# Key sums on TensorE and denominators read from PSUM for the first eight head pairs, in a plan where VectorE and GpSimd exclude each other

## The chip, the core and the metric

The kernel runs on one core of one Trainium2 chip. The metric is the device time of one execution in microseconds (us). Below, PE is TensorE, DVE is VectorE, ACT is ScalarE, POOL is GpSimd and SP is the engine whose queue issues the loads. SBUF is the working memory, PSUM the eight banks into which PE writes. "Pair" means two attention heads handled together.

## The reference

Linear attention with random features, and behind it a two-layer MLP; the MLP's weights arrive as 64-bit floats.

```python
q, k, v: [8, 8, 576, 64]        # batch, heads, sequence, head_dim; omega: [128, 64]

def phi(x):
    proj = np.einsum('bhsd,md->bhsm', x, omega)
    sq = np.sum(x * x, axis=-1, keepdims=True) / 2.0
    h = proj - sq
    h = h - np.max(h, axis=-1, keepdims=True)
    return np.exp(h) / np.sqrt(m)
q_p, k_p = phi(q_s), phi(k_s)                   # q, k scaled by 64**-0.25
kv = np.einsum('bhsm,bhsd->bhmd', k_p, v)
z = np.sum(k_p, axis=2)                         # the key sums
num = np.einsum('bhsm,bhmd->bhsd', q_p, kv)
den = np.einsum('bhsm,bhm->bhs', q_p, z)[..., None] + 1e-06
attn = num / den
x = attn.transpose(0, 2, 1, 3).reshape(4608, 512)
h = x @ w_in                                    # w_in [512, 2048]
out = (h / (1 + np.exp(-h))) @ w_out            # w_out [2048, 512]
```

## The kernel before

**Attention, one pair at a time (32 pairs, numbered n; four make a batch).** A pair's 1152 rows lie as nine chunks of 128: four of the first head, a middle chunk with 64 rows of each, four of the second. For keys and for queries PE projects the chunks into PSUM (`project`, L262, and the middle chunk apart, `project_mid`, L269). ACT squares the natural-layout copy and DVE sums it (`square_sum`, L254). DVE takes row maxima (`top`, L278 for four chunks, L276 for the middle one) and makes the shift (`shift`, L282 and L283, tiles `nbk` and `nbq`). ACT takes the exponential (L298).

**Key sums and denominators.** Before the change POOL adds the chunks of the exponentiated keys `hk` (`sums`, L318, L320, two of L323), PE adds over partitions with one product by a matrix of ones (`zsum`, L327), and ACT copies the result into SBUF as `zb` (`zcopy`, four copies). DVE multiplies `zb` with the exponentiated queries `hq` (`products`, L362, three instructions), sums the products (L369) and takes the reciprocal (L370). POOL scales the queries by it (`normal`, L375, three instructions), PE turns them (L381) and forms the numerators with the key-value matrix (`kv`, L343; `numer`, L399). ACT and DVE split the result into a high part `xh` (L413) and a low part `xl` (`x_low`, L418, two instructions, of 512 and of 64 columns). The pairs n < 8 (`DIRECT`) take their exponentials straight from PSUM.

**MLP.** There are nine row blocks t of 512 rows: the first 512 rows of each of the eight batches, and the remaining 64 of each together. Each block takes 16 steps f. A step is 12 products `x` by `w_in` into one bank (`stage1`, L495), two ACT instructions (L500, L501), one DVE subtraction (`g_low`, L505), and 12 products into four accumulator banks (`stage2`, L513). All of `stage1` of block 0 needs `xh` and `xl` of the pairs 0 to 3.

**Weights.** 32 tiles of weights are made from the 64-bit words. ACT makes the exponent part, DVE three instructions (`word`, L456, L458, L462, tile `w`), POOL two (`weight_high`, L476, and `weight_low`, L480). The step f of block 0 needs its own two tiles, so these 32 tiles are spread over the first part of the program.

**Order.** Each engine runs its instructions in the order written. That order comes from a list scheduler, `Plan.run`: each unit (a few instructions of one engine) has a duration, a key (its due time), the units that it comes after, and ring buffers and PSUM banks that it takes and frees. The scheduler repeatedly takes the unit that can start first, within 0.25 us the one with the lowest key. The PSUM banks are four `acc`, two `h` and two `att`. Before the MLP starts attention may use all of them; later only the two `att`:

```python
def bank_pools(u):
    pools = ["att"]
    if u["key"] < clock(LAG) - 1:
        pools.append("acc")
    if u["key"] < START_MLP - 1:
        pools.append("h")
```

Of the kernel before, what the change touches and what calls it, by code (L numbers as in the profile page):

```python
# [8 lines left out]
F32 = mybir.dt.float32  # L9
# [47 lines left out]
CALM = 0.5  # L57


def clock(step):  # L60
    return START_MLP + SLOW * min(step, 16) + STEP * max(step - 16, 0)


class Plan:
# [6 lines left out]
    def add(self, name, eng, dur, key, fn, after=(), order=(), alloc=(), free=(), banks=0, table=None, lat=0.0):  # L71
        u = dict(
            name=name, eng=eng, dur=dur, key=key, fn=fn, after=list(after), order=list(order), alloc=list(alloc),
            banks=banks, table=table, lat=lat,
        )
# [5 lines left out]
    def run(self):  # L81
        end, first = {}, {}
        slots = {r: [] for r in RINGS}
# [47 lines left out]
        while any(ready.values()):  # L131
            best = None
            for e, us in ready.items():
                pick, least = None, None
                for u in us:
# [21 lines left out]
                    t = max(t, free_at[e])  # L157
# [30 lines left out]
            order.append(u)  # L188
            for c in children.get(n, ()):
# [8 lines left out]
def attention_mlp(ctx: ExitStack, tc: tile.TileContext, qT, kT, qn, kn, v, om_in, w_in, w_out, out):  # L198
# [19 lines left out]
    prod = const.tile([P, NC, M + 1], F32, tag="prod", name="prod")  # L218
    nc.gpsimd.memset(prod, GUARD)
# [109 lines left out]

    def zcopy(n):  # L330
# [217 lines left out]
    for n in range(NWIN):  # L548
        calm = n < LEAD
        for i, who in enumerate("kq"):  # L550
# [6 lines left out]
            add(("raw",) + w, "SP", 0.42, at(n, i - 14, 8 + 10 * i - 32), lambda n=n, who=who: load_raw(n, who),  # L557
                order=prev("raw"), alloc=[(f"raw{who}", ("raw",) + w)], lat=1.3)
            before = [("nat", n, "k")] if i else ([("nat", n - 1, "q")] if n else [])
            add(("nat",) + w, "SP", 0.42, at(n, i - 13.5, 8.1 + 10 * i - 32), lambda n=n, who=who: load_nat(n, who),  # L560
# [3 lines left out]
            add(("ssum",) + w, "DVE", 0.78, at(n, 2 * i - 3, 14 + 10 * i - 32), lambda n=n, who=who: square_sum(n, who),  # L564
# [3 lines left out]
            add(pj, "PE", 1.5, at(n, 3 * i, o), lambda a, b, n=n, who=who: project(n, who, a, b), banks=2,  # L568
# [7 lines left out]
            for j in range(3):  # L576
                add(("top", n, who, j), "DVE", 0.3 if j == 2 else 0.7,
                    at(n, 3 * i + 1 + 0.1 * j, o + 1.2 + (4.5 if j == 2 else 0.1 * j)),
                    lambda n=n, who=who, j=j: top(n, who, j), after=[md if j == 2 else pj])
            if calm:  # L580
                add(("nb", n, who, 0), "DVE", 0.45, at(n, 3 * i + 1.5, 0), lambda n=n, who=who: shift(n, who, every),
                    after=[("top", n, who, j) for j in range(3)] + [("ssum",) + w], free=[("ss",) + w])
            else:
                add(("nb", n, who, 0), "DVE", 0.5, at(n, 0, o + 1.4), lambda n=n, who=who: shift(n, who, sides),
                    after=[("top", n, who, j) for j in range(2)] + [("ssum",) + w])
                add(("nb", n, who, 2), "DVE", 0.4, at(n, 0, o + 5.8), lambda n=n, who=who: shift(n, who, middle),
                    after=[("top", n, who, 2), ("ssum",) + w], free=[("ss",) + w])
# [15 lines left out]
        add(("v", n), "SP", 0.42, at(n, -8, 26 - 32), lambda n=n: load_v(n), order=[("v", n - 1)] if n else [],  # L603
            alloc=[("v", ("v", n))], lat=1.2)
# [3 lines left out]
        add(("sums", n), "POOL", 3.2, at(n, 6, 25), lambda n=n: sums(n), after=e["k"], order=[("sums", n - 1)] if n else [],  # L608
            alloc=[("t", ("t", n)), ("es", ("es", n))], free=[("h", n, "k"), ("t", n)])
        zn = ("z", n)  # L610
        add(zn, "PE", 0.45, at(n, 7, 32), lambda ps, n=n: zsum(n, ps), after=[("sums", n)], banks=1, free=[("es", n)])
        add(("zc", n), "ACT", 1.1, at(n, 7.1, 33.2), lambda n=n: zcopy(n), after=[zn], order=[("zc", n - 1)] if n else [],
            alloc=[("zb", ("zb", n))], free=[bk(zn)])
        merged = n > LEAD
        kn_ = ("kvnum", n - 1) if merged else ("kv", n)
        if not merged:
            add(("kv", n), "PE", 1.5, at(n, 6.5, 28.5), lambda ps, n=n: kv(n, ps), after=e["k"] + [("v", n)], banks=1,
# [3 lines left out]
        add(("ktt", n), "PE", 0.12, at(n, 6.7, 36.5), lambda ps, n=n: kv_turn(n, ps), after=[("kt", n)], banks=1,  # L621
# [3 lines left out]
        add(("prod", n), "DVE", 1.7, at(n, 8, 34.2), lambda n=n: products(n),  # L625
            after=e["q"] + [("zc", n)], order=[("den", n - 1)] if n else [], free=[("zb", n)])
        add(("den", n), "DVE", 1.6, at(n, 8.1, 34.4), lambda n=n: denom(n), after=[("prod", n)],
            alloc=[("den", ("den", n)), ("rd", ("rd", n))])
# [14 lines left out]
        dur = 1.4  # L643
        if follow:
# [3 lines left out]
            dur = 2.6  # L648
# [7 lines left out]
        add(("rest", n), "SP", 0.8, at(n, 20, 64), lambda n=n: keep_rest(n), after=[("xl", n, 0), ("xl", n, 1)], lat=0.2,  # L656
# [118 lines left out]
```

## Time and profile before

| | |
|---|---|
| device time, median of 3 runs | 1090.24 us (1089.62 to 1092.56) |
| profiled execution: its own time, its span | 1089.61 us, 1087.5 us |
| PE busy | 1040.2 us, 96% of the span |
| DVE, ACT, POOL busy | 572.1, 574.3, 254.6 us |
| the chain that ended last, by engine | PE 80%, DVE 9%, ACT 6%, DMA 2%, issue 2% |

The span runs from the first to the last instruction; 2.1 us of the execution's own time lie outside it. Busy time is an average over stages with different limits, so the stretches of the span are to be read one by one. Rows of the timeline give a start and a duration. Neighbouring rows of an engine overlap by some hundredths of a microsecond, so a cost in a row of instructions is best read from start to start.

### The profile page before, as it was taken

How to read it: one execution, taken by the hardware profiler on the slowest of the kernel's cores; microseconds unless marked ns; L12 is line 12 of the kernel's file. 1: busy time of each engine (PE TensorE's matmuls, PEld its weight loads, DVE VectorE, ACT ScalarE, POOL GpSimd, SP SyncE). 2: the span in 40 equal slices, each digit the busy share in tenths (PEclk: the TensorE clock that was granted, in tenths of full speed). 3: DMA queues.
4: the chain of work that ended last, by engine and by line, in shares of the span. 5: the costliest groups of instructions: out<-in, count | busy, mean ns of one | idle time of the engine just before them, and what ended most of it. 6: DMA issues, size and time to landing. Idle time of an engine off the chain costs nothing.

```text
span 1087.5 us, 16156 instructions
## 1 busy us (share of the span) xinstructions
PE 1040.2 (96%) x5900; PEld 825.2 (76%) x5900; DVE 572.1 (53%) x1109; ACT 574.3 (53%) x1077; POOL 254.6 (23%) x327
## 2 busy tenths in 40 slices
PE   5678998999999999999999999999999999999997
PEld 4456776677877778777877777777788778888886
DVE  6999988745555555545555555555555421111111
ACT  5677776565556555655556555655554543112111
POOL 3766655411222222121122211222222200000000
PEclk7868999999999999999999999999999999999999
DMA  7766777754435443544345444534442226333323
GB/s 274 248 220 228 271 249 243 238 176 141 141 123 176 128 126 118 175 141 130 123 133 172 126 136 141 180 122 137 130 157 89 65 83 213 97 97 126 107 97 97
DMA packets 66526, 167.84 MB, mean 154 GB/s; under 512 B 15632, under 2 KB 15760, under 8 KB 66448
## 3 DMA queue, kind: packets, MB, share of 16 engines
q1 hardware_dynamic: 65984, 166.23, 47.6%
q8 instruction: 47, 0.77, 0.3%
q10 hardware_dynamic: 464, 0.59, 0.2%
q14 instruction: 31, 0.25, 0.1%
HBM read 146.87 MB, written 19.92 MB: 153 GB/s over the span
## 4 chain that ended last, share of the span: by engine, by line
PE 80%; DVE 9%; ACT 6%; DMA 2%; issue 2%; POOL 0%; ACTq 0%; SPq 0%; DVEq 0%; POOLq 0%
PE ps_h L495 33%; PE ps_acc L513 32%; PE ps_att L262 5%; PE ps_att L343 3%; PE ps_att L381 2%; PE ps_att L399 2%; DVE w L458 1%; PE ps_att L327 1%; ACT L500 1%; DVE w L462 1%; PE ps_att L269 1%; DVE w L456 1%; DMA out<-ot 1%; DVE prod L362 1%; DMA wo_d<-wp 1%
## 5 line engine op out<-in xcount | busy, mean ns | idle before, releaser
L513 PE MATMUL ps_acc<-wo,gh 128*128 128x512 f32 x1152 | 369.0, 401 | 0.0
L500 ACT ACTIVATE gh<-ps_h 128x512 fp32r<-128x512 f32 x144 | 86.2, 599 | 308.4 <-PE ps_h L495 307.8
L505 DVE TENSOR_TENSOR gl<-ps_h,gh 128x512 fp32r<-128x512 f32 x144 | 97.9, 680 | 283.7 <-ACT ps_h L501 283.6
L513 PEld LDWEIGHTS ps_acc<-wo,gh 128*128 128x128 f32 x1152 | 206.2, 188 | 43.3
L495 PE MATMUL ps_h<-xh,wh 128*128 128x512 f32 x576 | 237.7, 413 | 0.3 <-ACT xh L413 0.3
L495 PE MATMUL ps_h<-xl,wh 128*128 128x512 f32 x576 | 225.5, 392 | 2.9 <-DVE xl L418 2.9
L495 PE MATMUL ps_h<-xh,wl 128*128 128x512 f32 x576 | 226.1, 393 | 0.0
L513 PE MATMUL ps_acc<-wo,gl 128*128 128x512 f32 x576 | 225.6, 392 | 0.0
L375 POOL TENSOR_TENSOR hq<-hq,rd 128x384 f32<-128x384 f32 x96 | 78.5, 846 | 380.0 <-DVE rd L370 375.3
L495 PEld LDWEIGHTS ps_h<-xh,wh 128*128 128x128 f32 x576 | 108.6, 189 | 24.8 <-ACT xh L413 0.5
L495 PEld LDWEIGHTS ps_h<-xl,wh 128*128 128x128 f32 x576 | 108.9, 189 | 24.1 <-DVE xl L418 3.3
L495 PEld LDWEIGHTS ps_h<-xh,wl 128*128 128x128 f32 x576 | 108.6, 188 | 24.5
L513 PEld LDWEIGHTS ps_acc<-wo,gl 128*128 128x128 f32 x576 | 108.1, 188 | 23.4
L318 POOL TENSOR_TENSOR t<-hk 128x256 f32<-128x256 f32 x64 | 48.8, 781 | 202.7 <-ACT hk L312 190.5
L312 ACT ACT_TABLE_LOAD x48 | 61.6, 1283 | 55.7 <-DVE hq L303 49.6
L501 ACT ACTIVATE ps_h<-ps_h 128x512 f32<-128x512 f32 x144 | 85.4, 593 | 0.0
L500 ACT ACT_TABLE_LOAD x56 | 71.8, 1283 | 22.7 <-PE ps_h L495 22.0
L278 DVE TENSOR_REDUCE mxq<-ps_att 128x4 f32<-128x512 f32 x57 | 36.9, 685 | 85.4 <-PE ps_att L262 85.4
L362 DVE TENSOR_TENSOR prod<-hq,zb 128x512 f32<-128x512 f32 (+1 forms) x96 | 53.0, 607 | 41.1 <-ACT zb L336 40.8
L250 ACT ACTIVATE nat<-nat 128x576 f32<-128x576 f32 x64 | 44.3, 700 | 23.4 <-DMA nat<-kn 18.6
L381 PE MATMUL ps_att<-ident,hq 128*128 128x128 f32 x261 | 41.0, 284 | 6.0 <-DVE hk L306 1.6
L278 DVE TENSOR_REDUCE mxk<-ps_att 128x4 f32<-128x512 f32 x55 | 35.5, 686 | 16.8 <-PE ps_att L262 16.8
(120 smaller groups left out, 1199.1 us busy)
## 6 DMA issues: line engine op xcount, KB each, us to landing
wo<-wo_d SPq DMA_DIRECT2D x144, 512.0 KB, 3.4
rawk<-kT SPq DMA_DIRECT2D x32, 352.0 KB, 3.0
rawq<-qT SPq DMA_DIRECT2D x32, 352.0 KB, 4.0
v<-v SPq DMA_DIRECT2D x32, 320.0 KB, 3.0
nat<-kn SPq DMA_DIRECT2D x32, 288.0 KB, 3.1
nat<-qn SPq DMA_DIRECT2D x32, 288.0 KB, 3.3
wraw<-w_in SPq DMA_DIRECT2D x16, 512.0 KB, 4.1
wraw<-w_out SPq DMA_DIRECT2D x16, 512.0 KB, 4.8
```

The costliest lines, as they stand in the source:

```text
L262: nc.tensor.matmul(ps[:, i * M : (i + 1) * M], raw[r, o : o + P], oms[r], start=True, stop=True)
L278: nc.vector.tensor_reduce(m[:, 5 * j : 5 * j + 4], ps.rearrange("p (c m) -> p c m", m=M), AX.X, ALU.max)
L312: nc.scalar.activation(h, h, AF.Exp)
L318: nc.gpsimd.tensor_tensor(t[:, j], e[:, 5 * j : 5 * j + 2], e[:, 5 * j + 2 : 5 * j + 4], ALU.add)
L362: nc.vector.tensor_tensor(prod[:, c, :M], e[:, c], zb[:, j].unsqueeze(1).broadcast_to([P, hi - lo, M]), ALU.mult)
L375: nc.gpsimd.tensor_tensor(e[:, c], e[:, c], rd[:, c].unsqueeze(2).broadcast_to([P, 3, M]), ALU.mult)
L381: nc.tensor.transpose(ps[:, i * P : (i + 1) * P], T["h", n, "q"][:, 3 * g + i], ident)
L495: nc.tensor.matmul(ph, w[:, k, :], x, start=k == 0 and n == 0, stop=k == NK - 1 and n == 2)
L500: nc.scalar.activation(gh, ph, AF.Silu)
L501: nc.scalar.activation(ph, ph, AF.Silu)
L505: nc.vector.tensor_tensor(gl, T["ph", t, f], T["gh", t, f].bitcast(F32), ALU.subtract)
L513: nc.tensor.matmul(T["po", t][j], g[:, js], w, start=f == 0 and n == 0, stop=f == NF - 1 and n == 2)
```

## The change

Four things change.

1. For the pairs n < 8, `sums`, `zsum` and `zcopy` are gone. `zsum_direct` lets PE sum the keys itself: ten products of 128x128 with ones (for the middle chunk with `sides_of`, ones in one half of the partitions) accumulate in one bank.
2. For the same pairs `denom_direct` replaces `products` and `denom`: ten times a product and a sum in one DVE operation, one input from SBUF and one straight from that PSUM bank. Each is two instructions in the built program, the operation and a read of its accumulator. The bank is freed when the last of them is done. For n >= 8 `denom` does nine of these with both inputs in SBUF, in place of three products and one sum.
3. The scheduler knows a "port": POOL's units and the DVE units marked `port` (the shifts, the weight words, the denominators of n >= 8) do not overlap in the plan. It also charges PE more after a gap. Many durations in its table are new.
4. `shift_keys` moves the keys of some early units by fixed pseudo-random amounts.

```diff
+SHIFTS = (1000, 1001, 1004, 1005, 1007, 1011, 1020, 1026, 1056, 1068, 1094, 1152, 1161,)
+def shift_keys(units):
+    early = [u for u in units if u["key"] < 235]
+    for seed in SHIFTS:
+        r = random.Random(seed)
+        part, wide = ((0.02, 6.0), (0.06, 3.0), (0.2, 1.5))[seed % 3]
+        for u, d in [(u, r.gauss(0, wide)) for u in early if r.random() < part]:
+            u["key"] += d
...
-                    t = max(t, free_at[e])
+                    t = max(t, free_at[e], port if u["port"] else 0.0)
...
+            if e == "PE":
+                if t - free_at[e] > 2.5:
+                    warm = t + 4.0
+                if t < warm:
+                    dur *= 1.7
             free_at[e] = t + dur
+            if u["port"]:
+                port = t + dur
...
-    prod = const.tile([P, NC, M + 1], F32, tag="prod", name="prod")
-    nc.gpsimd.memset(prod, GUARD)
+    sides_of = const.tile([P, 2, P], F32, tag="sides", name="sides")
+    nc.gpsimd.memset(sides_of, 0.0)
+    for j in range(2):
+        nc.gpsimd.memset(sides_of[j * D : (j + 1) * D, j], 1.0)
+    prod = const.tile([P, NC, M], F32, tag="prod", name="prod")
...
+    def zsum_direct(n, ps):
+        e = T["h", n, "k"]
+        for j in range(2):
+            nc.tensor.matmul(ps[:, j * M : (j + 1) * M], sides_of[:, j], e[:, MID], start=True, stop=False)
+            for i in range(4):
+                nc.tensor.matmul(ps[:, j * M : (j + 1) * M], ones, e[:, 5 * j + i], start=False, stop=i == 3)
+        T["z", n] = ps
+
+    def denom_direct(n):
+        e, z = T["h", n, "q"], T.pop(("z", n))
+        den = new("den", [P, NC])
+        for c in range(NC):
+            for j in range(2) if c == MID else [int(c > MID)]:
+                r = slice(j * D, (j + 1) * D) if c == MID else slice(0, P)
+                nc.vector.tensor_tensor_reduce(
+                    out=prod[r, c], in0=e[r, c], in1=z[r, j * M : (j + 1) * M], scale=1.0, scalar=GUARD, op0=ALU.mult,
+                    op1=ALU.add, accum_out=den[r, c : c + 1],
+                )
+        T["rd", n] = rd = new("rd", [P, NC])
+        nc.vector.reciprocal(rd, den)
...
-    def products(n):
+    def denom(n):
         e, zb = T["h", n, "q"], T.pop(("zb", n))
-        for j, (lo, hi) in enumerate(((0, 4), (4, 5), (5, 9))):
-            c = slice(lo, hi)
-            nc.vector.tensor_tensor(
-                prod[:, c, :M], e[:, c], zb[:, j].unsqueeze(1).broadcast_to([P, hi - lo, M]), ALU.mult
+        den = new("den", [P, NC])
+        for c in range(NC):
+            j = (c >= MID) + (c > MID)
+            nc.vector.tensor_tensor_reduce(
+                out=prod[:, c], in0=e[:, c], in1=zb[:, j], scale=1.0, scalar=GUARD, op0=ALU.mult, op1=ALU.add,
+                accum_out=den[:, c : c + 1],
             )
-
-    def denom(n):
-        den = new("den", [P, NC])
         T["rd", n] = rd = new("rd", [P, NC])
-        nc.vector.tensor_reduce(den, prod, AX.X, ALU.add)
         nc.vector.reciprocal(rd, den)
...
-            add(("ssum",) + w, "DVE", 0.78, at(n, 2 * i - 3, 14 + 10 * i - 32), lambda n=n, who=who: square_sum(n, who),
+            add(("ssum",) + w, "DVE", 0.76, at(n, 2 * i - 3, 14 + 10 * i - 32), lambda n=n, who=who: square_sum(n, who),
...
+        if n < DIRECT:
+            add(zn, "PE", 2.3, at(n, 6.2, 31), lambda ps, n=n: zsum_direct(n, ps), after=e["k"], order=[("mid", n, "q")],
+                banks=1, free=[("h", n, "k")])
...
+        if n < DIRECT:
+            add(("den", n), "DVE", 2.8, at(n, 8, 34.2), lambda n=n: denom_direct(n), after=e["q"] + [zn],
+                order=[("den", n - 1)] if n else [], alloc=[("den", ("den", n)), ("rd", ("rd", n))], free=[bk(zn)])
...
+    shift_keys(plan.units.values())
```

On POOL this is the program's start before, from the first key sums (`t`, `es`) on; `hq<-hq,rd` is the scaling of the queries, `wh`, `wl` and `wp` are the weight tiles.

```order
L318 TENSOR_TENSOR t<-hk 128x256 x2
L320 TENSOR_TENSOR es<-t 128x256
L323 TENSOR_TENSOR es<-es,hk 64x128 x2
L375 TENSOR_TENSOR hq<-hq,rd 128x384 x3
L476 CAST wh_324<-w_233 128x512
L480 TENSOR_TENSOR wl_325<-w_233,wh_324 128x512
L318 TENSOR_TENSOR t<-hk 128x256 x2
L320 TENSOR_TENSOR es<-t 128x256
L323 TENSOR_TENSOR es<-es,hk 64x128 x2
L476 CAST wh_404<-w_322 128x512
```

On POOL the same place now:

```order
L419 TENSOR_TENSOR hq<-hq,rd 128x384 x3
L520 CAST wh_312<-w_230 128x512
L524 TENSOR_TENSOR wl_313<-w_230,wh_312 128x512
L520 CAST wh_357<-w_306 128x512
L524 TENSOR_TENSOR wl_358<-w_306,wh_357 128x512
L520 CAST wp<-w_303 128x512
```

The key sums of the pairs have left POOL; scaling and weights follow each other directly.

On DVE this is the first pair's denominator before (`prod`, `den`, `rd`) and what follows it.

```order
L458 SCALAR_TENSOR_TENSOR w_233<-wre,w_233 128x512
L362 TENSOR_TENSOR prod<-hq,zb 128x4x128
L362 TENSOR_TENSOR prod<-hq,zb 128x128
L362 TENSOR_TENSOR prod<-hq,zb 128x4x128
L369 TENSOR_REDUCE den<-prod 128x9
L370 RECIPROCAL rd<-den 128x9
L254 TENSOR_REDUCE sqk<-nat 128x9
L282 TENSOR_TENSOR nbk<-mxk,sqk 128x9
L283 SCALAR_TENSOR_TENSOR nbk<-nbk,sqk 128x9
L254 TENSOR_REDUCE sqq<-nat 128x9
```

On DVE the end of the first pair's denominator now, and what follows it (`ps_att` is the PSUM bank with the key sums).

```order
L369 ISA prod,den<-hq,ps_att 128x128
L369 ISA den 128x1
L374 RECIPROCAL rd<-den 128x9
L303 TENSOR_REDUCE mxq<-ps_acc 128x4
L303 TENSOR_REDUCE mxq<-ps_h 128x4
L502 SCALAR_TENSOR_TENSOR w_230<-wre,w_230 128x512
L506 SCALAR_TENSOR_TENSOR w_230<-wraw,w_230 128x512
L279 TENSOR_REDUCE sqk<-nat 128x9
L307 TENSOR_TENSOR nbk<-mxk,sqk 128x9
```

The second pair's query maxima now stand behind the first denominator, and the two halves of a denominator's work (operation and accumulator read) alternate.

On PE this is the row from the fourth step of block 0 on in which the key sums of pair 5 stand now (`ps_att` from `hk`), between two quarters of a `stage2`.

```order
L557 MATMUL ps_acc<-wo,gl 128x512
L294 MATMUL ps_att<-oms,rawq 128x128
L358 MATMUL ps_att<-hk,sides 128x128
L360 MATMUL ps_att<-hk,ones 128x128 x4
L358 MATMUL ps_att<-hk,sides 128x128
L360 MATMUL ps_att<-hk,ones 128x128 x4
L557 MATMUL ps_acc<-wo,gh 128x512 x2
```

Five such groups of ten (pairs 0 to 4) stand ahead of the long run of `stage1` products that opens block 0, three (pairs 5 to 7) behind it.

## Rows read from the trace of the kernel before

**Rows 1.** Windows: stretch, busy us of each engine, PE clock, DMA share, GB/s.

```profile
0.00:90.00 90.00, 57.34 (x406) 41.03 (x407) 80.08 (x136) 59.42 (x178) 51.85 (x64) 0.75 0.74 250
90.00:210.00 120.00, 111.65 (x638) 85.65 (x639) 110.52 (x177) 85.42 (x170) 75.20 (x78) 0.99 0.74 248
210.00:1000.00 790.00, 789.28 (x4499) 630.99 (x4498) 370.16 (x780) 411.52 (x695) 127.52 (x187) 1.00 0.43 134
```

**Rows 2.** Timeline of DVE, first and last rows ahead of the long run.

```profile
5.66 0.75 DVE L254 TENSOR_REDUCE sqk<-nat 128x9 f32<-128x576 f32 x1 [4.66 <-ACT nat L250]
...
16.30 1.29 DVE L278 TENSOR_REDUCE mxq<-ps_acc 128x4 f32<-128x512 f32 x2 [2.01 <-PE ps_acc L262]
...
86.51 0.68 DVE L418 TENSOR_TENSOR xl<-ps_acc,xh 128x512 fp32r<-128x512 f32 x1
```

**Rows 3.** Timeline of POOL, one key sum and one weight.

```profile
10.86 0.72 POOL L318 TENSOR_TENSOR t<-hk 128x256 f32<-128x256 f32 x1 [8.59 <-ACT hk L298]
...
13.49 1.11 POOL L323 TENSOR_TENSOR es<-es,hk 64x128 f32<-64x128 f32 x2
...
26.02 1.59 POOL L480 TENSOR_TENSOR wl<-w,wh 128x512 fp32r<-128x512 f32 x1
```

**Rows 4.** Timeline of DVE beside those two.

```profile
10.96 0.65 DVE L282 TENSOR_TENSOR nbq<-mxq,sqq 128x9 f32<-128x9 f32 x1
...
26.52 1.64 DVE L462 SCALAR_TENSOR_TENSOR w<-wraw,w 128x512 uint32<-128x512 uint32 x1
```

**Rows 5.** Timeline of DVE, undisturbed: maxima and a shift.

```profile
8.85 0.28 DVE L276 TENSOR_REDUCE mxk<-ps_acc 128x1 f32<-128x128 f32 x1
9.16 0.17 DVE L282 TENSOR_TENSOR nbk<-mxk,sqk 128x9 f32<-128x9 f32 x1
...
9.45 1.28 DVE L278 TENSOR_REDUCE mxq<-ps_acc 128x4 f32<-128x512 f32 x2
10.65 0.28 DVE L276 TENSOR_REDUCE mxq<-ps_h 128x1 f32<-128x128 f32 x1
```

**Rows 6.** Timeline of DVE, undisturbed: one denominator.

```profile
18.52 1.50 DVE L362 TENSOR_TENSOR prod<-hq,zb 128x512 f32<-128x512 f32 x3
...
21.44 0.22 DVE L370 RECIPROCAL rd<-den 128x9 f32<-128x9 f32 x1
21.58 0.70 DVE L254 TENSOR_REDUCE sqk<-nat 128x9 f32<-128x576 f32 x1
```

**Rows 7.** Timeline of DVE, undisturbed: a low part and a sum of squares.

```profile
31.23 0.68 DVE L418 TENSOR_TENSOR xl<-ps_acc,xh 128x512 fp32r<-128x512 f32 x1
...
31.96 0.74 DVE L254 TENSOR_REDUCE sqk<-nat 128x9 f32<-128x576 f32 x1
32.62 0.67 DVE L278 TENSOR_REDUCE mxk<-ps_acc 128x4 f32<-128x512 f32 x1
```

**Rows 8.** Timeline of DVE, undisturbed: the three steps of a weight.

```profile
78.20 0.41 DVE L456 TENSOR_SCALAR w<-wraw 128x512 uint32<-128x512 uint32 x1
...
79.98 0.28 DVE L276 TENSOR_REDUCE mxq<-ps_att 128x1 f32<-128x128 f32 x1
```

**Rows 9.** Timeline of PE: products of 128x128, and the start of the long run.

```profile
11.86 2.40 PE L343 MATMUL ps_acc<-hk,v 128*64 128x128 f32 x20 [0.55 <-ACT hk L298]
...
34.12 0.49 PE L269 MATMUL ps_att<-oms,rawq 128*128 128x128 f32 x2
34.36 0.48 PE L495 MATMUL ps_h<-xh,wh 128*128 128x512 f32 x1
...
91.20 0.77 PE L495 MATMUL ps_h<-xh,wh 128*128 128x512 f32 x1
```

**Rows 10.** Timeline of PE: one key sum of before, and one `kv` later.

```profile
66.42 0.67 PE L327 MATMUL ps_att<-es,ones 128*128 128x256 f32 x2 [1.22 <-DVE xl L418]
66.93 0.39 PE L269 MATMUL ps_acc<-oms,rawk 128*128 128x128 f32 x2
...
144.44 1.31 PE L343 MATMUL ps_att<-hk,v 128*64 128x128 f32 x20
```

More of the change, by code (lines that the diff above doesn't have):

```diff
@@ L1 @@
+import random
 from contextlib import ExitStack
@@ L69, in __init__, with add @@
         self.freed_by = {}
-    def add(self, name, eng, dur, key, fn, after=(), order=(), alloc=(), free=(), banks=0, table=None, lat=0.0):
+    def add(self, name, eng, dur, key, fn, after=(), order=(), alloc=(), free=(), banks=0, table=None, lat=0.0, port=False):
         u = dict(
             name=name, eng=eng, dur=dur, key=key, fn=fn, after=list(after), order=list(order), alloc=list(alloc),
-            banks=banks, table=table, lat=lat,
+            banks=banks, table=table, lat=lat, port=port or eng == "POOL",
         )
@@ L79, in add, with run @@
             self.freed_by.setdefault(i, []).append(name)
-    def run(self):
+    def run(self, until=None):
         end, first = {}, {}
+        port, warm = 0.0, 0.0
         slots = {r: [] for r in RINGS}
@@ L188, in run @@
             order.append(u)
+            if n == until:
+                return t
             for c in children.get(n, ()):
@@ L580, in attention_mlp @@
             if calm:
-                add(("nb", n, who, 0), "DVE", 0.45, at(n, 3 * i + 1.5, 0), lambda n=n, who=who: shift(n, who, every),
-                    after=[("top", n, who, j) for j in range(3)] + [("ssum",) + w], free=[("ss",) + w])
-            else:
[L584 to L587, printed above, removed]
+                add(("nb", n, who, 0), "DVE", 0.36, at(n, 3 * i + 1.5, 0), lambda n=n, who=who: shift(n, who, every),
+                    after=[("top", n, who, j) for j in range(3)] + [("ssum",) + w], free=[("ss",) + w], port=True)
+            else:
+                add(("nb", n, who, 0), "DVE", 0.36, at(n, 0, o + 1.4), lambda n=n, who=who: shift(n, who, sides),
+                    after=[("top", n, who, j) for j in range(2)] + [("ssum",) + w], port=True)
+                add(("nb", n, who, 2), "DVE", 0.34, at(n, 0, o + 5.8), lambda n=n, who=who: shift(n, who, middle),
+                    after=[("top", n, who, 2), ("ssum",) + w], free=[("ss",) + w], port=True)
             for j in range(3):
@@ L655, in attention_mlp @@
                 lambda n=n, i=i: x_low(n, i), after=[("xh", n, i)], free=[bk(nm, i)])
-        add(("rest", n), "SP", 0.8, at(n, 20, 64), lambda n=n: keep_rest(n), after=[("xl", n, 0), ("xl", n, 1)], lat=0.2,
+        add(("rest", n), "SP", 0.75, at(n, 20, 64), lambda n=n: keep_rest(n), after=[("xl", n, 0), ("xl", n, 1)], lat=0.2,
             free=[("x", t, k)])
     def weight(i, key, src, last, more=()):
-        add(("wl",) + i, "SP", 0.42, key - 12, lambda: load_weight(src, i), order=[("wl",) + last] if last else [],
+        add(("wl",) + i, "SP", 0.36, key - 12, lambda: load_weight(src, i), order=[("wl",) + last] if last else [],
             alloc=[("wraw", ("wraw",) + i)], lat=2.1)
@@ L664, in weight @@
         for s in range(3):
-            add(("wd",) + i + (s,), "DVE", (0.5, 0.78, 0.75)[s], key - 2 + 0.1 * s, lambda s=s: word(i, s),
+            add(("wd",) + i + (s,), "DVE", (0.43, 0.7, 0.7)[s], key - 2 + 0.1 * s, lambda s=s: word(i, s),
                 after=([("wd",) + i + (s - 1,), ("re",) + i] if s else [("wl",) + i]),
@@ L680, in attention_mlp @@
         last = ("out", f)
-        add(("keep", f), "SP", 0.42, clock(f + LAG) + 4, lambda f=f: keep_weight(f), after=[("wlo", "out", f)], lat=2.1,
+        add(("keep", f), "SP", 0.36, clock(f + LAG) + 4, lambda f=f: keep_weight(f), after=[("wlo", "out", f)], lat=2.1,
             free=[("wp", f)])
```

48 lines of the change are left out of this document (24 added, 24 removed).

## Prediction

> **What bounds the kernel now.** I read the busy time by stretches first [rows 1]. From 210 us on PE is busy for 789.3 of 790 us: nothing that other engines do there can move the end. From 90 to 210 us it idles 8.35 us, and from 0 to 90 us 32.7 us, at a mean granted clock of 0.75. So only two things can change the time: the moment at which the long run of MLP products starts (91.20 us [rows 9]), and the work and gaps of PE behind it. Then I asked what holds that moment back. The run needs `xl` of pair 3, which DVE writes at 86.51 us [rows 2]; DVE is busy for 80.1 of the first 90 us [rows 1], and the longest wait in that stretch behind its first instruction is 2.0 us [rows 2]. The start is a queue of DVE instructions.
>
> That busy time isn't all work. The `shift` at 10.96 us takes 0.65 us and ends at 11.61, just behind POOL's addition that ends at 11.58; the same form takes 0.17 us when POOL rests [rows 3 to 5]. The weight word at 26.52 us takes 1.64 us; POOL's subtraction beside it runs until 27.61 [rows 3, 4], and what remains of the word behind that, 0.55 us, is less than the 0.6 or so that a quiet one takes. So some DVE operations stand still until POOL's current instruction is over, and this counts as busy. Reductions (0.60 us from start to start) and `xl` do not stretch.
>
> How much is it? By the written order, DVE does the following ahead of pair 3's `xl`, priced from start to start in quiet places [rows 5 to 8]: 13 sums of squares of 0.66, 22 maxima of 0.60, 10 middle maxima of 0.31, 13 shifts of 0.29, 9 weights of 1.78 and one first step more (0.45), 4 denominators of 3.06, one set of products (1.53), 3 low parts of 0.73: 61.1 us. It really takes 86.51 - 5.66 = 80.85 us, 2.0 of them idle. Some 17.7 us are collisions with POOL.
>
> **The change, part by part.**
>
> *DVE ahead of the long run.* The new order has ahead of pair 3's `xl`: 11 sums of squares, 20 maxima, 10 middle maxima, 11 shifts, 9 weights and 1.6 us of two begun ones, 3 low parts and a bit, 4 denominators. Without the denominators that is 7.3 + 12.0 + 3.1 + 3.2 + 17.6 + 2.3 = 45.5 us.
>
> A direct denominator is ten operations on 128 elements that read PSUM, ten accumulator reads and a reciprocal. No row shows the operation. Below stands the middle maximum, 128 elements from PSUM, started over 0.19 us if the next one needn't wait (0.31 less the wait), so 10 x 0.19 + 0.2 = 2.1 us. Above stands the same maximum at its full 0.28 us [rows 5] with 0.17 us for each read (the duration of an operation on nine elements [rows 5]) and a reciprocal: 10 x 0.45 + 0.2 = 4.7 us. I take 0.28 for each operation with its read hidden in the overlap, and 0.14 for the reciprocal (21.44 to 21.58 [rows 6]): 2.9 us, hardly less than the 3.06 of before. Four of them make 11.8 and the total 57.3 us. [...]
>
> *Collisions.* POOL's key sums go for pairs 0 to 4: one takes from 10.86 to 14.60 us [rows 3], five some 18.7 of POOL's 51.9 busy us [rows 1]. If collisions shrink with POOL's work, 17.7 becomes 11.3 us; if the new plan really keeps the two apart, 0. Nothing enforces the plan while it runs, so I take 6. The rows already show which operations are spared: the low part reads one input from PSUM and one from SBUF and keeps 0.68 us [rows 2, 7], the shift reads two from SBUF and stretches [rows 4]; the direct denominator is of the first kind. [...]
>
> *Waits.* With less of its own work DVE reaches operations whose input isn't ready. [...] I take 6 us for the idle of this stretch, between the 2 of now and 10.
>
> So `xl` of pair 3 starts at 5.66 + 57.3 + 6 + 6 = 75.0 instead of 86.5 us: 11.5 us earlier.
>
> *PE.* A product of 128x128 at the full clock takes 0.24 us from start to start (34.12 to 34.36 [rows 9]), ten 2.4 us; the key sum that goes took 0.51 (66.42 to 66.93 [rows 10]). Each pair costs PE 1.9 us more. Five of eight lie ahead of the long run, in the 32.7 idle us. Three lie behind it and count in full: 5.7 us. Six transposes also move behind the start, 0.8 us. Together 6.5 us later.
>
> *Gaps from 90 to 210 us.* The 8.35 us [rows 1] come from a DVE that is 92% busy there. Its 22 remaining weights and its shifts lose less to POOL, so gaps should shrink; against that, the bank with the key sums is now held until the denominator is done, and attention has two banks by then. Bounds: all 8.35 gone, or 6 us more (three pairs at 2). I take 4 us less.
>
> *What costs nothing.* ACT is spared four copies a pair and is 66% busy in the first 90 us. In the pairs n >= 8 DVE's denominators change, but DVE has 420 idle us of 790 there [rows 1]; cover gone, it would take some 17 us more per pair (420 over 24 pairs) before DVE were full. Loads: DMA works at a share of 0.74 for 90 us [rows 1]; the same bytes in 79 us ask 0.84, which leaves it the later bound. The three POOL fills of `sides_of` run in the first microseconds, where POOL rests until 10.86 [rows 3].
>
> **Sum.** Against the profiled execution: span 1087.5 - 11.5 + 6.5 - 4 = 1078.5 us, with the 2.1 us outside the span 1080.6. The median of the runs lies 0.6 us above that execution, so I forecast 1081 us, 0.8% faster. What this measurement can tell from no change is about 0.3%, 3.3 us: faster ends at 1087, slower begins at 1093.5.
>
> **The rivals.**
>
> *The collisions vanish* as planned and the gaps behind the start close: 6 + 4.35 us more, 1071 us. For it: each collision in the rows pairs a DVE operation with a POOL operation that the new order can set apart. Against it: order isn't time, and any late input shifts the two queues against each other.
>
> *The denominators are dear on DVE.* If each accumulator read costs its own start, four denominators take 7 us more: 1088 us. For it: five DVE instructions of a denominator become 21. Against it: small operations do overlap by some hundredths here.
>
> [...]
>
> **Chances and range.** 0.45 for my forecast (1075 to 1087), 0.17 for vanished collisions (1064 to 1075), 0.21 for dear denominators (1085 to 1092), 0.17 for a cold TensorE (1092 to 1100). Faster holds the first two and a quarter of the third, 0.67; same the rest of it and the edge of the last, 0.17; slower 0.16. The range from 1067 to 1095 leaves out about 0.05 below (all the low bounds at once) and 0.12 above.
>
> **What would show it.** Right: the long run starts at 77 to 82 us; shifts and weight words on DVE are near 0.17 and 0.42 to 0.69 us for the most part; the direct denominator takes some 2.9 us from its first operation to its reciprocal, whatever POOL does; PE's idle from the start to 210 us is near 4 us; the ten products take 2.4 us at the full clock. Wrong: DVE idle of over 10 us ahead of the start, with PE's key sums as what ended it (cold TensorE); denominators of over 4 us; weight words of over 0.9 us on average (the plan doesn't keep the engines apart); or idle on PE behind 210 us, where I assume none.

## The result and the profile after

The changed kernel takes 1076.95 us (median of 4 runs, 1074.47 to 1078.38). The kernel before takes 1090.94 us in the same comparison (1089.62 to 1092.56). The ratio is 0.9869, with a 95% interval from 0.9845 to 0.9893: 1.3% faster. The forecast was 1081 us, in a range from 1067 to 1095. The profiled execution after took 1076.36 us with a span of 1074.6 us; before, the span was 1087.5 us.

Over the whole span PE is busy for 6.5 us more than before (1046.7 instead of 1040.2 us) and idle for 19.4 us less (27.9 instead of 47.3 us). The windows of the kernel after answer to [rows 1]; the fourth line is the stretch from the new start of the long run to 210 us. Columns: stretch, its length, busy us of PE, PEld, DVE, ACT and POOL, each with its instructions, granted clock, DMA share, GB/s.

```profile
0.00:90.00 90.00, 71.24 (x562) 56.96 (x563) 79.78 (x234) 63.51 (x174) 38.96 (x48) 0.91 0.78 268
90.00:210.00 120.00, 116.25 (x695) 93.53 (x694) 91.73 (x234) 83.41 (x155) 55.64 (x57) 0.97 0.76 252
210.00:1000.00 790.00, 789.35 (x4484) 630.82 (x4483) 347.90 (x1090) 410.85 (x694) 125.83 (x184) 1.00 0.42 134
75.20:210.00 134.80, 129.01 (x763) 103.30 (x764) 106.16 (x269) 97.31 (x185) 64.86 (x66) 0.97 0.73 243
```

PE does 71.2 us of work in the first 90 us instead of 57.3, at a granted clock of 0.91 instead of 0.75. Behind 210 us nothing changed. DVE is as busy in the first 90 us as before, but gets much further in them, and POOL has 12.9 us less to do. The chain that ended last now lies on PE for 90%, by engine (before: PE 80%, DVE 9%, ACT 6%):

```profile
PE 90%; DVE 4%; ACT 2%; DMA 1%; issue 1%; POOL 0%; ACTq 0%; SPq 0%; DVEq 0%
```

The timeline of DVE after shows the first denominator (its first operation and the first read of its accumulator, then its reciprocal and the row behind), and the low part of pair 3.

```profile
14.15 0.29 DVE L369 CUSTOM_DVE_ANT_0 prod<-hq,ps_att 128x128 f32<-128x128 f32 x1 [0.88 <-ACT hq L323]
14.36 0.08 DVE L369 DVE_READ_ACCUMULATOR2_ANT den<- 128x1 f32 x1
...
16.57 0.22 DVE L374 RECIPROCAL rd<-den 128x9 f32<-128x9 f32 x1
16.70 0.63 DVE L303 TENSOR_REDUCE mxq<-ps_acc 128x4 f32<-128x512 f32 x1
...
72.63 0.68 DVE L462 TENSOR_TENSOR xl<-ps_att,xh 128x512 fp32r<-128x512 f32 x1
```

A denominator takes 16.70 - 14.15 = 2.55 us. Its operations start 0.21 us apart though each is shown with 0.28 us, and the reads of the accumulator lie inside that overlap. The low part starts at 72.63 instead of 86.51 us [rows 2].

The timeline of PE after has the key sums of the first pair, at a granted clock of 1.00, those of the second, and the start of the long run. Two groups of ten products are shown, each from its first row to the row behind it; the last row is the first product of the run.

```profile
11.52 0.46 PE L358 MATMUL ps_att<-hk,sides 128*128 128x128 f32 x2 [0.65 <-ACT hk L323]
...
13.92 0.33 PE L389 MATMUL ps_acc<-hk,v 128*64 128x128 f32 x2
...
26.10 0.63 PE L358 MATMUL ps_acc<-hk,sides 128*128 128x128 f32 x2
...
29.66 0.65 PE L443 MATMUL ps_att<-en,kw 128*64 128x512 f32 x2
...
75.20 0.48 PE L539 MATMUL ps_h<-xh,wh 128*128 128x512 f32 x1
```

Ten products took 2.40 us at 11.52, and 3.56 us at 26.10, where the stretch from 20 to 30 us has a granted clock of 0.57. Taken in stretches of 1 us, the clock shows two levels in this trace, 1.00 in 1045 and 0.50 in 21 of 1075, and something between in nine; from 20 to 28 us it is 0.50. The long run starts at 75.20 us, 16.0 us earlier [rows 9]. From there to the end it now takes 999.4 us, before 996.3. The windows from the start of the long run to the end, before and after:

```profile
91.20:1087.50 996.30, 981.68 (x5491) 783.27 (x5489) 490.86 (x973) 514.44 (x899) 201.52 (x263) 1.00 0.46 146
```

```profile
75.20:1074.60 999.40, 988.18 (x5552) 791.58 (x5552) 464.06 (x1375) 522.70 (x906) 190.69 (x250) 1.00 0.46 146
```

PE works 6.5 us longer there and idles 3.4 us less (11.2 instead of 14.6 us).

Does DVE still collide with POOL? Rows of POOL after, and below them rows of DVE beside them.

```profile
29.20 1.60 POOL L524 TENSOR_TENSOR wp<-w,wp 128x512 fp32r<-128x512 f32 x1
...
45.59 0.61 POOL L520 CAST wp<-w 128x512 fp32r<-128x512 f32 x1 [2.01 <-DVE w L506]
46.28 1.29 POOL L524 TENSOR_TENSOR wp<-w,wp 128x512 fp32r<-128x512 f32 x1
```

```profile
29.70 1.65 DVE L506 SCALAR_TENSOR_TENSOR w<-wraw,w 128x512 uint32<-128x512 uint32 x1
...
45.65 0.28 DVE L369 CUSTOM_DVE_ANT_0 prod<-hq,ps_acc 128x128 f32<-128x128 f32 x1
...
47.10 0.28 DVE L369 CUSTOM_DVE_ANT_0 prod<-hq,ps_acc 128x128 f32<-128x128 f32 x1
```

The weight word at 29.70 us waits out POOL's subtraction, 1.65 us instead of 0.69. The denominator from 45.44 us on runs through two POOL instructions, and each of its operations keeps 0.28 us.

I went through all rows of DVE up to 210 us in this way. A row counts as beside POOL if at least a tenth of it overlaps a row of POOL, and what it takes over its quiet duration (0.17 for a shift, 0.41, 0.69 and 0.69 for the words of a weight, 0.51 on average for a product of the old denominator) is its stretch. The sums are worked out from the two timelines:

| | rows that can stretch | of these beside POOL | stretch up to 210 us | ahead of pair 3's low part |
|---|---|---|---|---|
| before | 179 | 112 | 42.9 us | 17.7 us |
| after | 156 | 61 | 21.2 us | 9.1 us |

The first word of a weight has a single input in SBUF, and it stretches too: here (first DVE, then POOL) it takes 1.51 us instead of 0.41, beside a subtraction of POOL that ends at 127.26.

```profile
126.03 1.51 DVE L500 TENSOR_SCALAR w<-wraw 128x512 uint32<-128x512 uint32 x1
```

```profile
125.64 1.62 POOL L524 TENSOR_TENSOR wl<-w,wh 128x512 fp32r<-128x512 f32 x1
```

Of the 80 direct operations, 21 lie beside POOL. They take 0.282 us on average, and the 59 others take 0.283 us.

### The profile page after: what moved, and what is told of

It reads as the page before. It is cut to its first block, busy times and chain, and to the rows that moved or that the text cites. A ratio compares the mean times of both kernels' runs of the same rounds, so it can differ in the third digit from the quotient of the medians.

```text
span 1074.6 us, 16797 instructions
## 1 busy us (share of the span) xinstructions
PE 1046.7 (97%) x6044; PEld 838.8 (78%) x6044; DVE 529.4 (49%) x1573; ACT 572.3 (53%) x1049; POOL 220.4 (21%) x289
## 4 chain that ended last, share of the span: by engine, by line
PE 90%; DVE 4%; ACT 2%; DMA 1%; issue 1%; POOL 0%; ACTq 0%; SPq 0%; DVEq 0%
PE ps_acc L557 37%; PE ps_h L539 36%; PE ps_att L287 5%; PE ps_att L389 3%; PE ps_att L425 3%; PE ps_att L443 2%; PE ps_att L294 1%; DVE prod L369 1%; PE ps_att L352 1%; PE ps_att L360 1%; DVE w L502 1%; DMA wo<-wo_d 1%; DMA rawq<-qT 0%; ACT hk L323 0%; PE ps_acc L287 0%
## 5 line engine op out<-in xcount | busy, mean ns | idle before, releaser
L343 POOL TENSOR_TENSOR t<-hk 128x256 f32<-128x256 f32 x48 | 34.4, 738 | 199.1 <-ACT hk L337 199.1
L409 DVE CUSTOM_DVE_ANT_0 prod<-hq,zb 128x128 f32<-128x128 f32 x216 | 47.8, 288 | 38.9 <-ACT zb L382 38.9
L275 ACT ACTIVATE nat<-nat 128x576 f32<-128x576 f32 x64 | 44.4, 697 | 14.6 <-DMA nat<-kn 10.5
L429 ACT COPY en<-ps_att 128x384 f32<-128x384 f32 x89 | 40.5, 480 | 7.0 <-PE ps_att L425 5.4
```

The source lines that it names most:

```text
L275: nc.scalar.activation(nat, nat, AF.Square, scale=SCALE * 0.5**0.5)
L409: nc.vector.tensor_tensor_reduce(out=prod[:, c], in0=e[:, c], in1=zb[:, j], scale=1.0, scalar=GUARD, op0=ALU.mult, op1=ALU.add, accum_out= ...
L429: nc.scalar.copy(T["en", n][:, 3 * g * P : 3 * (g + 1) * P], T.pop(("t", n, g))[:, : 3 * P])
```

## The experiments

Each was run in five rounds against the kernel before, whose median was 1089.62, 1089.55 and 1088.70 us in the three groups of runs. So ratios are compared. "Start" is the start of pair 3's low part on DVE (before 86.51 us), "idle" that of PE from 90 to 210 us (before 8.35 us). The stretch is that of the rows named above; fused operations with both inputs in SBUF, which it leaves out, add 1.5 us in e3n and 2.3 us in e5n.

| | us | ratio to before | start | idle | stretch up to 210 us |
|---|---|---|---|---|---|
| the change | 1076.95 | 0.9869 (0.9845 to 0.9893) | 72.63 | 3.75 | 21.2 |
| e1 new operations, old plan | 1085.16 | 0.9956 (0.9939 to 0.9973) | 75.05 | 7.1 | 25.8 |
| e2 without shift_keys | 1083.76 | 0.9948 (0.9931 to 0.9965) | 73.87 | 6.5 | 21.8 |
| e9 without it and without port | 1080.98 | 0.9928 (0.9910 to 0.9945) | 80.6 | 6.3 | 24.4 |
| e3n without it, key sums on POOL | 1090.83 | 1.0016 (1.0006 to 1.0027) | 78.0 | 13.2 | 27.6 |
| e5n without it, direct for n < 5 | 1085.13 | 0.9964 (0.9951 to 0.9976) | 73.0 | 11.6 | 28.2 |
| e8n without it, sums copied to SBUF | 1079.37 | 0.9908 (0.9891 to 0.9925) | 80.6 | 3.7 | 22.8 |
| e4 before, shorter key sums | 1081.65 | 0.9924 (0.9906 to 0.9943) | 81.30 | 5.1 | 28.5 |
| e7 the change, idle work on POOL | 1080.22 | 0.9917 (0.9903 to 0.9930) | 75.38 | 5.5 | 27.7 |
| e10 before, idle work on PE | 1098.85 | 1.0090 (1.0076 to 1.0103) | 89.96 | 10.3 | 41.0 |

My theory was that POOL's key sums hold up DVE, and DVE the long run. Its rivals were that the plan, not the operations, brings the gain; that the shorter way to the denominator alone brings it; and that TensorE's clock does. The times of e2, e3, e4, e7, e8n and e10 fell into none of the ranges that I had written down for them.

**e1: the operations without the plan.** The new operations, with the scheduler, the durations and the keys of before. Two of the lines in which it differs from the changed kernel; the gap rule and the new durations are gone as well.

```diff
-                    t = max(t, free_at[e], port if u["port"] else 0.0)
+                    t = max(t, free_at[e])
...
-    shift_keys(plan.units.values())
```

> The new operations in the scheduler of before: key sums by TensorE and direct denominators for the first eight pairs, but no port rule, no gap rule, no shifted keys and the old durations for everything that is not new. If the gain comes from taking the key sums off GpSimd (five of 3.7 us ahead of the long run, so about a third fewer collisions and a shorter way to each denominator), the long run of MLP products starts at 80 to 86 us instead of 91.2 and the time is 1081 to 1087 us. If the gain comes from the new order alone, the start stays near 90 us and the three late key sums on TensorE make it 1094 to 1097 us.

The start came to 75.05 us, nearly where the whole change has it. But only a third of the gain in time came with it. PE idles 7.1 us from 90 to 210 us and 4.9 us from 210 to 1000 us (after: 3.75 and 0.65), in the later stretch for low parts of DVE alone (the time in total, the number of waits and the longest):

```profile
PE ps_att L330 <- DVE xl L440: 4.9, 5, 2.3
```

PE is also busy for 3.9 us longer than after (1050.6 us), although its mean clock is higher (0.992 instead of 0.988); why stays open.

**e2: the plan without the shifted keys.**

```diff
-    shift_keys(plan.units.values())
```

> The changed kernel without the shifted keys; port rule, gap rule and durations stay. If operations and port rule carry the gain, the start of the long run moves by at most 4 us from 75.2 and the time is 1075 to 1082 us. If the shifted keys carry it (an order tuned unit by unit), the start is at 84 us or later and the time 1086 us or more.

0.52% faster than before instead of 1.31%. So 0.8% hang on the shifted keys, more than half of the gain, although the start is only 1.2 us later. The windows of this run, the first from its start of the long run on:

```profile
75.95:210.00 134.05, 126.63 (x729) 99.06 (x727) 105.67 (x269) 91.92 (x172) 66.59 (x69) 0.96 0.73 244
...
210.00:1000.00 790.00, 788.33 (x4492) 629.97 (x4493) 350.41 (x1100) 411.06 (x693) 126.19 (x185) 1.00 0.42 135
```

Over its whole span of 1083.3 us PE idles 27.5 us, as after (27.9), but is busy for 9.1 us longer on the same 6044 instructions. Most of that goes with the clock: PE is busy for 31.4 us at the lower of the two levels, 0.50, after for 18.1 us. In the key sum at 26.10 us after, instructions start every 0.21 us at that level and every 0.11 us at 1.00, so 13.3 us more at the lower level cost some 6 us, as an estimate. In the stretches around its waits (PE busy for 7.98 of 10 us from 140 on and 7.18 from 160 on) and just behind them the granted clock is 0.80 to 0.86 in three of four slices. The remaining 3 us I can't place. Nor is the clock all of it: of the six executions of e2 the one with the highest mean clock (0.991) takes 1081.54 us, and the slowest of the change, at 0.987, takes 1078.38 us.

shift_keys draws its numbers in the order of the early units. Where a variant adds or takes away units, the same seeds move other keys. Three kernels (e3, e5 and e8) were first run with shift_keys left in; their shifts are therefore others than those of the change (in e5 for the units listed behind those of pair 4), and they were repeated without it, to stand against e2.

**e3 and e3n: the plan without the operations' key part.** POOL sums the keys of all pairs, and denominators read two inputs from SBUF.

```diff
+DIRECT_Z = 0
...
-        if n < DIRECT:
+        if n < DIRECT_Z:
             add(zn, "PE", 2.3, at(n, 6.2, 31), lambda ps, n=n: zsum_direct(n, ps), after=e["k"], order=[("mid", n, "q")],
```

> The changed kernel with the key sums of all pairs back on GpSimd, copied to SBUF by ScalarE, and nine fused operations per denominator; port rule, gap rule, durations and shifted keys stay. TensorE has 5.7 us less to do behind the start of the long run. If taking the key sums off GpSimd is what brings the start forward, it is at 81 us or later and the time is 1078 to 1086 us. If the plan's port rule is enough, the start stays at 75 to 78 us and the time is 1069 to 1074 us, better than the changed kernel.

With shift_keys: 1090.69 us, ratio 1.0008 (0.9995 to 1.0022), slower than either range; the low part of pair 3 starts at 83.30 us.

> Key sums of all pairs on GpSimd in the new plan, without the shifted keys: it differs from the kernel without the shift (1083.76 us) in the new operations alone. If GpSimd's key sums cost VectorE time, it is 6 us or more slower than that, 1090 us or more, with the low part of pair 3 at 80 us or later, as the run with a shift of other units suggested (1090.69 us, 83.30 us). If that run was slow because its shifted keys fell on other units, it is at 1080 to 1086 us.

Without: 1090.83 us, 0.7% slower than e2. The new plan alone gains nothing. It does avoid collisions (27.6 us of stretch instead of 42.9), but pays for them in waits:

```profile
0.00:90.00 90.00, 67.60 (x456) 49.85 (x457) 69.31 (x210) 65.92 (x195) 48.49 (x68) 0.85 0.70 230
90.00:210.00 120.00, 106.79 (x574) 82.00 (x572) 98.16 (x207) 77.02 (x147) 71.13 (x75) 0.93 0.76 255
```

DVE, busy for 69.31 of 90 us, now stands idle for 20.7 us where it was idle for 9.9 [rows 1], and PE has 13.2 us of gaps behind 90 us. This run also shows what no row of before did, the fused operation with two inputs from SBUF beside POOL (first DVE, then POOL):

```profile
139.86 0.28 DVE L410 CUSTOM_DVE_ANT_0 prod<-hq,zb 128x128 f32<-128x128 f32 x1
...
140.91 1.36 DVE L410 CUSTOM_DVE_ANT_0 prod<-hq,zb 128x128 f32<-128x128 f32 x1
```

```profile
140.70 1.42 POOL L525 TENSOR_TENSOR wl<-w,wh 128x512 fp32r<-128x512 f32 x1
```

The same operation takes 0.28 us in quiet and 1.36 us beside POOL's subtraction, until just behind the end of that at 142.12.

**e4: only POOL's key sums shorter.** The kernel before, in its own order; POOL does one of the five additions of a key sum and leaves out the rest, so most chunks are missing from the sums, for all pairs.

```diff
-        t = new("t", [P, 2, 2, M])
-        for j in range(2):
-            nc.gpsimd.tensor_tensor(t[:, j], e[:, 5 * j : 5 * j + 2], e[:, 5 * j + 2 : 5 * j + 4], ALU.add)
...
-        nc.gpsimd.tensor_tensor(es, t[:, :, 0], t[:, :, 1], ALU.add)
-        for j in range(2):
-            r = slice(j * D, (j + 1) * D)
-            nc.gpsimd.tensor_tensor(es[r, j], es[r, j], e[r, MID], ALU.add)
+        nc.gpsimd.tensor_tensor(es, e[:, 0:2], e[:, 5:7], ALU.add)
```

> The kernel before, with the same order on every engine, but GpSimd's key sums cut from five instructions (some 3.3 us of work) to one of 0.73 us; it leaves out most chunks of the key sums. If collisions between VectorE and GpSimd set the start of the long run, they shrink from 17.7 us by about a quarter and the start comes 4 to 7 us earlier: 1083 to 1087 us. If GpSimd's work is beside the path, the start stays at 91 us and the time at 1089 to 1092 us.

8 us faster, with no instruction moved on any engine. The stretch ahead of the start fell from 17.7 to 10.9 us and the start from 86.51 to 81.30 us, as expected; the time fell further than expected, for PE's idle time from 90 to 210 us shrank as well, from 8.35 to 5.1 us. Here the sum is ready sooner too, so e7 puts the work back without that.

**e7: the change with idle work on POOL.** Five additions on constants, in the sizes of the old key sum, behind the third scaling of each pair n < 8; nothing uses them.

```diff
+        if n < DIRECT and g == 2:
+            for _ in range(3):
+                nc.gpsimd.tensor_tensor(spare, sides_of, sides_of, ALU.add)
+            for j in range(2):
+                r = slice(j * D, (j + 1) * D)
+                nc.gpsimd.tensor_tensor(spare[r, j], spare[r, j], ones[r], ALU.add)
```

> The changed kernel, same order on every engine, with five idle-work instructions of GpSimd (the shapes of the key sums, on constants) behind the third scaling of each of the first eight pairs. Nothing waits for their results, so the way from keys to denominator is as short as in the changed kernel; only GpSimd's port is busy 3.3 us more per pair and the weights behind it are later. If collisions are what the key sums cost, the weight words and shifts on VectorE stretch again and the time is 1081 to 1087 us. If it was the length of the way through GpSimd, TensorE and ScalarE, the time stays at 1075 to 1079 us.

0.5% slower than the change by the ratios, the start 2.75 us later, 6.5 us more stretch up to 210 us. The time lies between the two ranges, nearer to the one for collisions. PE, ACT and DVE keep the order of the change, and ahead of the start DVE's waits did not grow (1.7 us in those of over 0.15 us, after 2.65) while its stretch did, from 9.1 to 13.4 us. So POOL's work costs through DVE even where nothing waits for it, though less than e4 gave back (0.76%).

**e9: the plan without the port.**

```diff
-            banks=banks, table=table, lat=lat, port=port or eng == "POOL",
+            banks=banks, table=table, lat=lat, port=False,
...
-    shift_keys(plan.units.values())
```

> The changed kernel without the rule that GpSimd and the marked VectorE work exclude each other in the plan, and without the shifted keys, so that it stands against the kernel without the shift alone (1083.76 us). If the rule keeps the engines apart on the chip, more VectorE time goes to collisions without it: the low part of pair 3 starts at 77 us or later and the time is 1086 us or more. If the new operations alone bring the early start, as the kernel with the old plan suggests (start of that low part at 75.05 us), the low part starts at 72 to 75.5 us and the time is within 3 us of 1083.8.

Neither expectation came true as a whole: the start is late (80.6 us), and yet the time is not worse than that of e2. The rule saves 2.6 us of stretch up to 210 us, and the time shows none of it. How early the long run starts does not say by itself what a plan is worth.

**e8 and e8n: denominators with both inputs in SBUF.** PE sums, ACT copies the sums, DVE does nine operations.

```diff
+            add(("zc", n), "ACT", 1.0, at(n, 7.1, 33.2), lambda n=n: zcopy(n), after=[zn], order=[("zc", n - 1)] if n else [],
+                alloc=[("zb", ("zb", n))], free=[bk(zn)])
...
-        if n < DIRECT:
+        if n < 0:
             add(("den", n), "DVE", 2.8, at(n, 8, 34.2), lambda n=n: denom_direct(n), after=e["q"] + [zn],
```

> The changed kernel with key sums on TensorE for the first eight pairs, but copied to SBUF by ScalarE, and nine fused operations with two SBUF inputs each in place of ten with one from PSUM; the bank is freed by the copies. If one input from PSUM matters because such an operation doesn't collide with GpSimd, denominators here take 3 us or more where GpSimd works, the start is 2 to 5 us later and the time 1079 to 1085 us. If it doesn't matter, the denominators take 2.3 to 2.5 us and the time is 1075 to 1079 us.

With shift_keys: 1083.82 us, ratio 0.9950 (0.9937 to 0.9962).

> Key sums by TensorE, but copied to SBUF by ScalarE, and denominators of two inputs from SBUF; without the shifted keys, against the kernel without the shift (1083.76 us). If denominators with two inputs from SBUF collide with GpSimd as shifts and weight words do, eight of them lose some 0.6 us or more each, and the low part of pair 3 comes 2 us or more later than without (73.9 us): 1086 us or more. If they do not collide, the nine operations instead of ten and the copies by ScalarE leave it within 2 us of 1083.8.

Without: 1079.37 us, 0.4% faster than e2 and than I had expected either way, although the start is as late as the first expectation had it. In this plan all 81 operations up to 210 us fell into pauses of POOL (0.288 us each), so the sensitive form cost nothing. (With shift_keys two of 81 lay beside POOL and took 0.65 us on average.) So a plan of this kind can be as fast without a denominator that reads PSUM.

**e5 and e5n: the last three key sums back on POOL**, with denominators of two inputs from SBUF for these three pairs.

```diff
+DIRECT_Z = 5
...
-        if n < DIRECT:
+        if n < DIRECT_Z:
```

> The changed kernel with key sums on TensorE and direct denominators for the pairs 0 to 4 only; the pairs 5 to 7, behind the start of the long run, get their key sums on GpSimd again. The start stays at 75 to 77 us and TensorE has 5.7 us less behind it. If the stretch behind the start is bound by TensorE's own work, the time falls by 3 to 6 us against the changed kernel, to 1071 to 1075 us. If GpSimd's three key sums bring their collisions and gaps back there, as they did for the version with all sums on GpSimd, the time is 1077 us or more.

With shift_keys: 1081.36 us, ratio 0.9928 (0.9916 to 0.9941), 0.6% slower than the change. PE keeps the order of the change up to 81 us and the start is as early (72.02 us), but PE idles 10.6 us from 90 to 210 us instead of 3.75.

> TensorE's key sums for the pairs 0 to 4 alone, without the shifted keys, against the kernel without the shift (1083.76 us). If the three key sums that lie behind the start of the long run cost their 5.7 us of TensorE in full, as the prediction has it, and the gaps stay, it is at 1078 us. If TensorE's saving is given back as idle time behind the start, because GpSimd has key sums again between 90 and 210 us, it is at 1082 to 1087 us with over 9 us of idle time in that stretch.

Without: 1085.13 us, not faster than e2 (0.9964 against 0.9948). PE is spared three key sums, but idles 11.6 us from 90 to 210 us instead of 6.5, and the stretch up to 210 us is 28.2 us instead of 21.8. The three late key sums on TensorE cost nothing net; on POOL they cost as much or more.

**e10: a warmer TensorE.** The kernel before, with ten products of constants, which nothing uses, ahead of the key sums of the pairs 0 to 4.

```diff
+        for _ in range(10 if n < 5 else 0):
+            nc.tensor.matmul(ps[:, :M], ones, ident, start=True, stop=True)
```

> The kernel before, same order, with ten products of constants (128x128) on TensorE ahead of the key sum of each of the pairs 0 to 4: TensorE has the work of the changed kernel ahead of the long run, but the key sums stay on GpSimd. If the changed kernel gains because a busier TensorE is granted a higher clock in the first 90 us, the mean clock there rises from 0.75 to 0.85 or more and the time falls to 1080 to 1087 us. If the start is set by VectorE and GpSimd alone, the time is 1088 to 1093 us whatever the clock.

```profile
0.00:90.00 90.00, 62.98 (x503) 48.97 (x503) 75.60 (x130) 57.09 (x175) 49.26 (x62) 0.85 0.73 241
```

The granted clock of the first 90 us rose from 0.75 to 0.85, the start came 3.5 us later and the kernel got 0.9% slower, more than either range allows. But the clock didn't rise alone: the idle products stand in front of each key sum, and DVE now waits for the sum's copy `zb` where it hardly did before [rows 6]:

```profile
19.20 1.49 DVE L364 TENSOR_TENSOR prod<-hq,zb 128x512 f32<-128x512 f32 x3 [1.59 <-ACT zb L338]
...
36.66 1.49 DVE L364 TENSOR_TENSOR prod<-hq,zb 128x512 f32<-128x512 f32 x3 [1.85 <-ACT zb L338]
```

So the run shows that a PE with this much more work, and the higher clock that came with it, does not bring the gain; what the clock alone is worth it doesn't show.

## Why the prediction came out right

**The bound.** Right: the start was a queue of DVE instructions, partly standing still beside POOL. The 17.7 us of collisions that I worked out by subtraction are 17.7 us when summed row by row, closer than the subtraction deserves: it counted 2.0 us of idle time and left out 0.6 us at 8.18 us. e4, which takes POOL work away, gave 8 us, and e7, which puts work back that nothing waits for, took 0.5%.

**DVE ahead of the long run.** Forecast: low part of pair 3 at 75.0 us; measured 72.63. The denominators took 2.53 to 2.55 us, not 2.9: the distance between starts, 0.21 us, was the price, and I had taken the duration, 0.28. That is 1.7 us over four (10.1 instead of 11.8). Collisions were 9.1 us, not 6. Waits behind the first instruction were 0.41 + 0.88 + 0.68 + 0.68 = 2.65 us, not the 6 of my estimate, which no run shows: the key sums on PE are mostly in time. Together these are -1.7 + 3.1 - 3.4 = -2.0 of the 2.4 us; the other 0.4 us I can't place. The plan keeps the two engines apart in part only: up to 210 us the shifts average 0.29 us (median 0.17) and the three words of a weight 0.51, 0.88 and 0.85 us (medians 0.42, 0.69 and 0.69), the last two just short of my sign of being wrong (0.9).

The direct form is spared by POOL, as I argued from the low part: 21 operations beside POOL take 0.282 us on average, the 59 others 0.283 us. With both inputs in SBUF the same operation took 1.36 us beside POOL instead of 0.28 (e3n). A single input in SBUF isn't by itself what spares an operation, though: the first word of a weight has only one, and at 126.03 us it took 1.51 us instead of 0.41. What sets it apart from the direct form, no run here shows. And e8n shows that a plan can be fast without the spared form.

**From the low part to the run.** I assumed 4.7 us as before; it is 2.57 us (72.63 to 75.20). With it the start is 16.0 us earlier instead of 11.5.

**PE and the gaps.** Forecast behind the start: 6.5 us of work more, 4 us of gaps less, +2.5 us. Measured: 6.5 us of work more and 3.4 us of gaps less, +3.1 us. That the work comes out to the tenth is partly luck: the granted clock from the start to 210 us is 0.97 instead of 0.99, a loss of some 2 us, as an estimate, that my sum didn't have. PE idles 5.8 us from the start to 210 us, where I expected near 4. Its longest waits there:

```profile
PE ps_att L397 <- DVE xl L462: 2.0, 1, 2.0
PE ps_acc L557 <- ACT hk L323: 1.8, 1, 1.8
PE ps_acc L557 <- DMA wo<-wo_d: 1.4, 1, 1.4
```

The columns are the time in total, the number of waits and the longest. Once, for 2 us, PE still waits for DVE.

**The sum and its parts.** Span forecast 1078.5, measured 1074.6 us. What I did not see is where the parts come from. I priced the plan through collisions and gaps, and gave `shift_keys` no term at all. The experiments divide the 1.31% otherwise: the operations in the old plan give 0.44% (e1), in the new plan without shifts 0.68% (e3n against e2); the port, the gap rule and the new durations nothing that shows (e1 against e2; the port alone, e9 against e2); the shifted keys 0.79%. My sum in fact describes e2, which has the operations and the plan but not the keys, and its 1083.76 us lie in the range too, by two errors that partly cancel. There the long run starts 15.25 us earlier, not 11.5, and takes 11.0 us longer behind that, not 2.5: the work of PE grew by 11.8 us and its gaps shrank by 0.7. So the small net sum behind the start was right for this one set of keys, and that is luck. The variants with key sums on TensorE and other keys lie at 0.9908 to 0.9964 of before (e1, e2, e5, e5n, e8, e8n, e9).

**The rivals.** *Collisions vanish*: no, 9.1 us remain, and e9 shows that the rule for the port saves only 2.6 us of stretch. *Dear denominators*: no, 2.55 us. *Cold TensorE*: no. The 1092 to 1100 us were my estimate, and no run of the changed kernel shows them. Ten products were slow at least twice (3.56 us at 26.10 and 3.15 us at 57.65, against 2.40 us at a granted clock of 1.00), but the granted clock of the first 90 us rose to 0.91, and ahead of the start DVE waited for key sums only 0.7 us in one place.

**Open.** What the shifted keys improve is known by its place only in part: 0.75 us at the start of the long run and, in the profiled executions, some 6 us through the granted clock; some 3 us of PE's busy time are unexplained, and so is why these keys and not others do it. What the shorter way to the denominator is worth by itself no run shows: e4 holds it together with the collisions.

## What to carry to other kernels

Busy time of a full engine can be waiting in disguise, here 17.7 of DVE's 80.85 us ahead of the low part: price each form of instruction in a quiet place, sum the rest, and test it by cutting the other engine's work without moving anything, as e4 does. Here moving work off POOL was worth the 1.9 us a pair that it cost PE; forbidding the overlap in the plan only turned collisions into idle time while POOL kept its work (e3n: stretch 27.6 instead of 42.9 us, DVE idle for 20.7 instead of 9.9 of the first 90 us). In an order found by a scheduler, variants of one kernel scatter by half a per cent through their order alone, so a small edit has to be compared with its neighbours without chosen keys, and a moment of start is no measure of the end.

## What the hardware showed that I had not expected

The fused product and sum on DVE starts every 0.21 us for 128 elements, whether its second input comes from PSUM or, where POOL rests, from SBUF (e8n), and its accumulator read of 0.08 us lies in the overlap of two operations; behind the two operations of 64 partitions the next start comes after 0.30 and 0.31 us (medians). A shift of nine elements, 0.17 us in quiet, took 1.14 us beside a POOL subtraction (after, at 21.27 us, beside 21.12 to 22.38). And in these rows one collision costs up to the whole rest of POOL's instruction, so a short operation loses more, for its size, than a long one: this shift took 6.7 times its quiet time, the weight word of 1.65 us 2.4 times.
